# Sequential writes of the dilated heads' x, dilated masks spread on ScalarE, and a new table of due times

## The chip, the cores and the metric

The kernel runs on one core of a Trainium2 chip. The time is the device time of one execution in microseconds (us), lower is better; several executions are timed and their median is given. The engines are TensorE (PE; its weight loads are listed as PEld), VectorE (DVE), ScalarE (ACT), GpSimd (POOL) and SyncE (SP, which here issues the DMAs).

## The reference

Eight batches of 576 tokens, eight heads of 64. Heads 0 to 3 attend to a plain window of the last 32 tokens; heads 4 to 7 are dilated: they attend to every fourth token of the last 128. The concatenated heads go through a feed-forward block with a gate made by a three-tap convolution over tokens. All of it is float32.

```python
mask_plain = (rel >= 0) & (rel < 32)
mask_dil = (rel >= 0) & (rel < 128) & (rel % 4 == 0)
attn = softmax(where(mask, q @ k.T / 8, -1e9))
x = concat_heads(attn @ v)                 # (8, 576, 512)
h = relu(x @ w_in)                         # (8, 576, 1024)
gate = sigmoid(conv3(h, conv_w))           # taps at s-1, s, s+1
out = (h * gate) @ w_out                   # (8, 576, 512)
```

## The kernel before

**Attention.** A batch has four pairs of heads, p = 0 to 3; pairs 0 and 1 are plain (kind 0), pairs 2 and 3 dilated (kind 1). The host sorts the tokens of a dilated head by residue modulo 4, so that its window too becomes 32 neighbours. For a pair, `scores` (L255) issues 72 small matmuls into the PSUM buffer `att`, which is one buffer of four banks for the whole kernel; the add of the mask (L266) takes the scores out to SBUF, the softmax follows on VectorE and ScalarE (L268 to L289), a 32x32 transpose (L291) makes `pt`, and `values` (L307) issues 80 or 84 small matmuls into `att` again. `att` is free for the next pair when x has been taken out of it.

**Taking x out.** x is kept as two float32r tensors: x.t[0], names x0a to x6a in the trace, is the rounded value, and x.t[1], x0b to x6b, the rest. The cast at L330 (ACT) writes x.t[0] from PSUM. The rest is made in one of two ways. In batches 0 and 1 (`HELPED`), `less` (L334, PE) subtracts x.t[0] inside PSUM by matmuls with minus the identity, and a second ACT cast (L337) takes the difference out. In batches 2 to 7 one DVE subtraction (L342) reads PSUM and x.t[0] and writes x.t[1]. `made` gives the access patterns of all three. For a plain pair both sides are sequential. For a dilated pair PSUM holds the tokens by residue (four runs of 144) while x is in token order: the instruction walks PSUM in sequence and writes x in steps of four elements, 16 bytes.

**Feed-forward.** `expert` computes h by 192 matmuls of 288 columns per batch (L367), relu on ACT (L374), the convolution and the gate on ACT and DVE (L385, L379, L390, L392), splits the product in two (L394, L396), and multiplies by w_out with 512 columns (L412; 256 columns in batch 0); ACT copies the result (L422), SP stores it. Batches 0 and 1 take their exponentials slot by slot on ACT (L275, nine instructions a pair).

**Weights.** The weights arrive as 64-bit patterns in eight chunks (four of w_in, four of w_out) and `weights` converts each, with seven instructions on DVE and two on ACT (L476 to L491). PE can't begin a chunk of w_in before it is converted.

**Order.** `Planner` lays out all work before the kernel runs. Each step has an engine, a cost by the planner's own table and a due time from `DUE`. The planner repeatedly takes the engine that could start earliest and, of the steps that could start within 0.25 us of that, the one with the smallest due time. The order of instructions on each engine, SP's DMA queue included, is the sorted result. The planner's cost of a cast at L330 or L337 is 0.68 us and of the subtraction at L342 0.77 us, for plain and dilated pairs alike. `filled` puts matmuls of no use (L525) into PE's planned gaps between 5 and 31.5 us.

**Masks.** Before the planned work, small masks arrive by DMA (L497) and are spread over nine slots into `mask_sb` on DVE (L506 to L509), for both kinds.

Of the kernel before, what the change touches and what calls it, by code (L numbers as in the profile page):

```python
# [58 lines left out]
SCALE = 1.0 / D ** 0.5  # L59
SLOTS, HELPED = 0xff, 0xff  # L60
DUE = {
    "first": (157.10, 134.80, 52.00, 206.80, 505.80, -99.10, 677.00, 54.50),
    "gated": (199.50, 332.40, -57.10, -17.00, -100.80, -92.00, 541.40, -54.90),
    "second": (76.20, 952.70, 279.50, 455.50, 621.50, 924.90, 920.10, 207.80),
    "weights": (1282.30, 361.60, 883.70, 117.70, 161.40, 234.00, 242.00, 0.70),
    "fetch": (181.50, 89.90, 96.50, -94.10, 210.30, 760.90, 907.20, 915.10),
    "conv": 0.90,
    "scores": ((862.30, -93.20, -28.60, 858.10), (1.90, -187.00, -117.60, 119.50), (-13.20, 593.20, 765.10, 63.20), (141.00, -102.40, 265.70, -1.00), (184.00, 330.80, 18.90, 456.80), (229.10, 111.10, 305.10, 505.80), (620.00, 511.00, 783.60, 607.50), (932.70, -2.80, 494.20, 164.10)),
    "softmax": ((-34.40, -169.10, 49.00, 76.50), (-106.80, 15.70, 1.40, 96.40), (820.40, 925.10, 959.00, -67.90), (242.40, 566.70, -28.10, 230.90), (-66.40, 446.20, 40.30, 279.70), (632.70, 448.70, 871.10, -122.60), (592.80, -17.20, 875.60, -148.20), (-7.70, -174.00, 316.30, -52.10)),
    "values": ((120.70, -126.80, 16.90, -89.00), (-21.60, 21.90, -71.90, 35.70), (-22.30, -58.00, 92.90, -102.10), (140.70, -22.10, 73.40, 61.70), (468.60, 85.70, 99.50, 82.30), (184.50, -47.10, 183.70, 270.40), (284.30, 58.50, -77.80, 437.30), (-172.90, -95.90, 812.20, 434.80)),  # L70
    "queries": ((-134.90, -184.70, -104.20, -95.90), (-122.50, 4.80, 51.10, -59.30), (85.10, 70.50, -17.00, 144.40), (174.70, 186.60, 120.20, 157.10), (366.00, 234.00, 390.50, 255.70), (520.50, 532.70, 519.50, 248.70), (514.80, 543.20, 658.00, 446.80), (929.60, 882.70, 580.50, 835.90)),
    "runs": ((-56.90, -52.20, -66.80, -93.30), (68.20, -9.80, -23.30, -29.60), (80.40, 9.90, 147.40, 389.10), (498.10, 248.90, 25.00, 430.20), (635.00, 776.10, 449.50, 589.20), (922.60, 831.10, 869.40, 436.50), (1013.20, 1032.10, 1022.60, 620.40), (1268.60, 782.50, 987.10, 989.90)),
}


# [110 lines left out]
def attn_moe(ctx: ExitStack, tc: tile.TileContext, qk_p, qk_d, v_p, v_d, w_in, w_out, conv, mask, out):  # L186
    nc = tc.nc
# [49 lines left out]
    def attention(b, p):  # L237
        due, soft, val = SCORES[b][p], SOFTMAX[b][p], VALUES[b][p]
        kind = p // 2
        qk, v, s, m, z, pt, x = (Buffer(n) for n in ("qk", "v", "s", "m", "z", "pt", "x"))  # L240
# [3 lines left out]
            out=qk.t, in_=(qk_p, qk_d)[kind][b, p % 2]), uses=[qk])  # L244
        lv = plan.add("SP", 1.35, RUNS[b][p], lambda: nc.sync.dma_start(
            out=v.t, in_=(v_p, v_d)[kind][b, p % 2]), uses=[v])

        def scores():
# [18 lines left out]
            out=flat(), in0=scored(), in1=masked, op=ALU.add), [last], [sc, s])  # L267
        last = plan.add("DVE", 0.755, soft + 0.5, lambda: nc.vector.tensor_reduce(  # L268
            out=m.t, in_=flat(), axis=AX.X, op=ALU.max, negate=slotwise), [last], [s, m])
# [10 lines left out]
        else:  # L280
            last = plan.add("DVE", 0.755, soft + 1.0, lambda: nc.vector.tensor_tensor(
                out=flat(), in0=flat(), in1=wide(m.t), op=ALU.subtract), [last], [s, m])
            last = plan.add("ACT", 0.685, soft + 1.5, lambda: nc.scalar.activation(
                out=flat(), in_=flat(), func=AF.Exp, scale=SCALE), [last], [s], "exp")

            last = plan.add("DVE", 0.765, soft + 2.0, lambda: nc.vector.tensor_reduce(  # L286
                out=z.t, in_=s.t, axis=AX.X, op=ALU.add), [last], [s, z])
        last = plan.add("DVE", 0.215, soft + 2.2, lambda: nc.vector.reciprocal(out=z.t, in_=z.t), [last], [z])
        last = plan.add("DVE", 0.755, soft + 2.3, lambda: nc.vector.tensor_tensor(  # L289
            out=flat(), in0=flat(), in1=wide(z.t), op=ALU.mult), [last], [s, z])  # L290
        last = plan.add("DVE", 0.775, soft + 3.0, lambda: nc.vector.transpose(  # L291
            out=pt.t.rearrange("p (a k) -> p a k", k=W), in_=flat()), [last], [s, pt])
# [22 lines left out]
        def made(t):  # L315
            whole = tv.t.rearrange("p (c m) -> p c m", c=2)[:, :, TV0:TV0 + 2 * RUN]
            if kind == 0:
                return t.rearrange("p (c m) -> p c m", c=2), whole
            return t.rearrange("p (m c r) -> p c r m", c=2, r=2), whole.rearrange("p c (r m) -> p c r m", r=2)

        def spans():

            if kind == 0:
# [4 lines left out]
                    for c in range(2) for o, m, n in ((0, 0, RUN), (RUN, 0, 16), (RUN + 16, 16, RUN - 16))]  # L328

        last = plan.add("ACT", 0.68, val + 1.0, lambda: nc.scalar.copy(out=made(x.t[0])[0], in_=made(x.t[0])[1]), [last], [tv, x])  # L330
        if HELPED >> (b * NP + p) & 1:
            def less():
                for o, a in spans():
                    nc.tensor.matmul(tv.t[:, o:o + a.shape[1]], minus, a, start=False, stop=True, skip_group_check=True)  # L334

            last = plan.add("PE", 0.5, val + 1.2, less, [last], [tv, x], "E")
            return [plan.add("ACT", 0.68, val + 1.5, lambda: nc.scalar.copy(  # L337
                out=made(x.t[1])[0], in_=made(x.t[1])[1]), [last], [tv, x])]

        def low():  # L340
            out, whole = made(x.t[1])
            nc.vector.tensor_tensor(out=out, in0=whole, in1=made(x.t[0].bitcast(F32))[0], op=ALU.subtract)  # L342
# [153 lines left out]
    kinds_sb = cs[0][0].bitcast(BF16)[:, 0:5 * W].rearrange("p (a k) -> p a k", k=W)  # L496
# [5 lines left out]

    spread = lambda i, n: kinds_sb[:, i, :].unsqueeze(1).to_broadcast([128, n, W])
    slot_masks = [mask_sb[:, kind, :].rearrange("p (a k) -> p a k", k=W) for kind in range(2)]
    for t in slot_masks:
        nc.vector.tensor_copy(out=t, in_=spread(1, 9))  # L506
    nc.vector.tensor_copy(out=slot_masks[0][:, 0, :], in_=kinds_sb[:, 0, :])
    nc.vector.tensor_copy(out=slot_masks[1][:, 0, :], in_=kinds_sb[:, 2, :])
    nc.vector.tensor_copy(out=slot_masks[1][:, 4:6, :], in_=kinds_sb[:, 3:5, :])  # L509
    for t, in ss:  # L510
        nc.gpsimd.memset(t[:, :, W:W + 1], 1e-9)
    for h, in hs:
# [82 lines left out]
```

## Time and profile before

| | us |
|---|---|
| median of 3 runs (lowest to highest) | 525.82 (525.22 to 526.34) |
| the profiled execution, own time | 525.44 |
| its span, first to last instruction | 523.6 |
| busy PE / PEld / DVE / ACT in the span | 505.0 / 438.8 / 397.2 / 310.7 |

The span is taken from the profiled execution, whose own time is 1.84 us longer than its span and 0.38 us under the median. Busy times count an engine as busy while an instruction of it runs; matmuls are pipelined, so a busy PE isn't PE at its peak. The chain of waits is followed back from the last instruction to what released each step.

### The profile page before, as it was taken

The page shows a single profiled execution, that of the slowest core. Times are in us where ns is not written, and L with a number is a line of the kernel's source. Part 1 is how long each engine was busy: PE and PEld are TensorE (multiplying, and loading weights), DVE is VectorE, ACT ScalarE, POOL GpSimd, SP SyncE. Part 2 cuts the span into 40 slices and gives each one's busy share as a digit, 9 for nine tenths or more (in the row PEclk, how much of TensorE's full clock was granted, in tenths as well). Part 3 has the DMA queues.
Part 4 walks back from the last instruction along what each step waited for, and adds up shares of the span by engine and source line. Part 5 has one row for each costly group of instructions (what it writes and reads, how often), then busy time and mean ns, then how long its engine had stood idle before and what let it go on. Part 6 is the DMA issues. An engine that isn't in the chain of part 4 may idle for free.

```text
span 523.6 us, 16676 instructions
## 1 busy us (share of the span) xinstructions
PE 505.0 (96%) x7541; PEld 438.8 (84%) x7541; DVE 397.2 (76%) x555; ACT 310.7 (59%) x619; POOL 1.4 (0%) x27
## 2 busy tenths in 40 slices
PE   5989989999999999999999999999999999999996
PEld 3568889999777997799878998789977799789985
DVE  4998889998986899549992899957998469327900
ACT  4978989748423885268731787348733378338710
POOL 1000000000000000000000000000000000000000
PEclk9999989999999999999999999999999999999999
DMA  7766540211255004211333332230143200110011
GB/s 296 277 216 234 188 141 30 94 42 45 93 168 183 31 1 161 103 50 49 105 130 111 111 129 79 80 140 2 48 144 124 101 1 1 41 41 1 1 50 52
DMA packets 16551, 50.99 MB, mean 97 GB/s; under 512 B 2016, under 2 KB 3168, under 8 KB 15456
## 3 DMA queue, kind: packets, MB, share of 16 engines
q1 hardware_dynamic: 16336, 49.84, 28.0%
q8 instruction: 59, 0.97, 0.8%
q10 hardware_dynamic: 144, 0.08, 0.1%
q14 instruction: 12, 0.10, 0.1%
HBM read 40.48 MB, written 9.44 MB: 95 GB/s over the span
## 4 chain that ended last, share of the span: by engine, by line
PE 78%; DVE 12%; ACT 8%; DMA 1%; issue 1%; DVEq 0%; ACTq 0%
PE mm L367 35%; PE nn L412 32%; PE att L307 5%; PE att L255 4%; DVE s L289 2%; DVE pt L291 1%; DVE m L268 1%; DVE s L266 1%; PE nn L367 1%; DMA qk<-in_qk_p_dram 1%; DVE z L286 1%; ACT c L390 1%; PE att L334 1%; ACT h L374 1%; ACT L390 1%
## 5 line engine op out<-in xcount | busy, mean ns | idle before, releaser
L412 PE MATMUL nn<-wo,g 128*128 128x512 f32 (+1 forms) x960 | 211.9, 374 | 0.5 <-DVE g L396 0.3
L412 PEld LDWEIGHTS nn<-wo,g 128*128 128x128 f32 x960 | 163.7, 188 | 32.1 <-ACT g L394 0.7
L379 DVE SCALAR_TENSOR_TENSOR c<-h,conv_sb,c 128x576 f32<-128x576 f32 x128 | 102.9, 814 | 27.4 <-ACT c L385 25.9
L374 ACT ACTIVATE h<-mm 128x288 f32<-128x288 f32 x120 | 48.2, 407 | 34.4 <-PE mm L367 34.1
L422 ACT COPY out<-nn 128x512 f32<-128x512 f32 (+1 forms) x40 | 21.8, 544 | 65.6 <-PE nn L412 62.7
L367 PE MATMUL mm<-x0a,wi 128*128 128x288 f32 x208 | 59.1, 299 | 0.4 <-ACT h L374 0.4
L392 DVE TENSOR_TENSOR c<-c,h 128x576 f32<-128x576 f32 x64 | 47.9, 756 | 8.5 <-ACT c L390 8.0
L394 ACT CAST g<-c 128x576 fp32r<-128x576 f32 x64 | 42.8, 672 | 18.9 <-DVE c L392 18.8
L396 DVE TENSOR_TENSOR g<-c,g 128x576 fp32r<-128x576 f32 x64 | 47.6, 755 | 4.2 <-ACT g L394 2.8
L367 PE MATMUL mm<-x1a,wi 128*128 128x288 f32 x176 | 50.0, 300 | 0.2 <-ACT h L374 0.2
L385 ACT ACTIVATE c<-h,conv_sb 128x576 f32<-128x576 f32 x64 | 49.1, 777 | 1.5
L390 ACT ACTIVATE c<-c 128x576 f32<-128x576 f32 x64 | 43.2, 683 | 6.7 <-DVE c L379 5.7
L307 PEld LDWEIGHTS att<-pt,v 32*64 32x64 f32 x2624 | 31.5, 133 | 13.4 <-issue 4.4
L255 PEld LDWEIGHTS att<-qk 64*32 64x32 f32 x2304 | 26.5, 108 | 17.3 <-DMA qk<-in_qk_p_dram 5.3
L367 PEld LDWEIGHTS mm<-x0a,wi 128*128 128x128 f32 x208 | 39.0, 188 | 1.7 <-ACT h L374 1.3
L255 PE MATMUL att<-qk 64*32 64x64 f32 x2304 | 31.7, 230 | 7.5 <-DMA qk<-in_qk_p_dram 5.3
L307 PE MATMUL att<-pt,v 32*64 32x64 f32 (+1 forms) x2624 | 35.1, 233 | 2.7 <-DVE x5b L342 0.9
L266 DVE TENSOR_TENSOR s<-att,mask_sb 128x576 f32<-128x576 f32 x32 | 24.0, 751 | 17.9 <-PE att L255 17.8
L367 PE MATMUL mm<-x5a,wi 128*128 128x288 f32 x128 | 35.9, 295 | 0.0
L367 PE MATMUL mm<-x4a,wi 128*128 128x288 f32 x128 | 35.9, 295 | 0.0
L367 PEld LDWEIGHTS mm<-x1a,wi 128*128 128x128 f32 x176 | 33.0, 188 | 1.5 <-ACT h L374 0.9
L367 PE MATMUL mm<-x2a,wi 128*128 128x288 f32 x112 | 31.5, 297 | 0.0
(122 smaller groups left out, 813.2 us busy)
## 6 DMA issues: line engine op xcount, KB each, us to landing
qk<-in_qk_p_dram SPq DMA_DIRECT2D x16, 592.0 KB, 4.0
qk<-in_qk_d_dram SPq DMA_DIRECT2D x16, 592.0 KB, 4.1
out_dram<-out SPq DMA_DIRECT2D x28, 256.0 KB, 2.2
v<-in_v_d_dram SPq DMA_DIRECT2D x16, 384.0 KB, 3.7
v<-in_v_p_dram SPq DMA_DIRECT2D x16, 384.0 KB, 3.6
raw<-in_w_in_dram SPq DMA_DIRECT2D x4, 1024.0 KB, 6.4
raw<-in_w_out_dram SPq DMA_DIRECT2D x4, 1024.0 KB, 7.3
out_dram<-out SPq DMA_DIRECT2D x16, 128.0 KB, 2.4
```

The lines of the kernel that those rows point to most:

```text
L255: nc.tensor.matmul(sc.t[quad * 32:quad * 32 + 32, o:o + W], qk.t[hd * 64:hd * 64 + 64, q0:q0 + 32], qk.t[hd * 64:hd * 64 + 64, S + q0:S + ...
L266: last = plan.add("DVE", 0.75, soft + 0.0, lambda: nc.vector.tensor_tensor(out=flat(), in0=scored(), in1=masked, op=ALU.add), [last], [sc, s])
L307: nc.tensor.matmul(tv.t[hd * 64:hd * 64 + 64, o:o + hi - lo], v.t[quad * 32:quad * 32 + 32, i, hd * 64:hd * 64 + 64], pt.t[quad * 32:quad ...
L367: nc.tensor.matmul(ps.t[:, 0:HALF], wi[jw][fc // 2][:, fc % 2, k], x[k].t[jx][:, hf * HALF:hf * HALF + HALF], start=(k == 0 and i == 0), s ...
L374: relu.append(plan.add("ACT", 0.4, due + 1.6 * u + 1.6, lambda fc=fc, hf=hf, ps=ps: nc.scalar.activation(out=h[fc].t[:, 1 + hf * HALF:1 + ...
L379: nc.vector.scalar_tensor_tensor(out=c[fc].t, in0=h[fc].t[:, k:S + k], scalar=conv_sb[:, k, fc:fc + 1], in1=c[fc].t, op0=ALU.mult, op1=ALU ...
L385: t = plan.add("ACT", 0.777, d, lambda fc=fc: nc.scalar.activation(out=c[fc].t, in_=h[fc].t[:, 1:S + 1], func=AF.Copy, scale=conv_sb[:, 1, ...
L390: t = plan.add("ACT", 0.686, d + 1.0, lambda fc=fc: nc.scalar.activation(out=c[fc].t, in_=c[fc].t, func=AF.Sigmoid), [t], [c[fc]], "sigmoid")
L392: t = plan.add("DVE", 0.755, d + 1.5, lambda fc=fc: nc.vector.tensor_tensor(out=c[fc].t, in0=c[fc].t, in1=h[fc].t[:, 1:S + 1], op=ALU.mult ...
L394: hi = plan.add("ACT", 0.675, d + 2.0, lambda fc=fc: nc.scalar.copy(out=half(fc, 0), in_=c[fc].t), [t, *(done[fc] if odd else [])], [c[fc] ...
L396: lo = plan.add("DVE", 0.755, d + 2.5, lambda fc=fc: nc.vector.tensor_tensor(out=half(fc, 1), in0=c[fc].t, in1=half(fc, 0).bitcast(F32), o ...
L412: nc.tensor.matmul(ps.t[:, 0:n], g[k // 2].t[:, k % 2, jg, c0:c0 + 128], w.rearrange("p h c -> p (h c)") if hf is None else w[:, hf], star ...
```

## The change

Three edits. In `made` the dilated pattern turns its loops: x is walked in sequence (token group m, bank half c, residue r) and PSUM in steps: two elements 144 apart, then the same in the other bank half, then on to the next m. The three users of `made`, L330, L337 and L342, change with it; L334 doesn't. Second, the spreading of the masks is split: the plain masks stay on DVE (two instructions), the dilated ones (three instructions) go to ACT. Third, every value of `DUE` is new; no cost in the planner changes.

```diff
 DUE = {
-    "first": (157.10, 134.80, 52.00, 206.80, 505.80, -99.10, 677.00, 54.50),
+    "first": (74.70, 81.70, 357.10, 189.80, 929.80, 83.60, 71.70, 1180.10),
...
-    "weights": (1282.30, 361.60, 883.70, 117.70, 161.40, 234.00, 242.00, 0.70),
-    "fetch": (181.50, 89.90, 96.50, -94.10, 210.30, 760.90, 907.20, 915.10),
-    "conv": 0.90,
+    "weights": (82.70, 1550.20, 2380.40, 91.90, 97.30, -18.10, 171.90, 69.10),
+    "fetch": (69.90, 42.80, -64.40, -60.40, 72.60, 97.70, 1233.60, 1550.60),
+    "conv": 351.60,
...
             if kind == 0:
                 return t.rearrange("p (c m) -> p c m", c=2), whole
-            return t.rearrange("p (m c r) -> p c r m", c=2, r=2), whole.rearrange("p c (r m) -> p c r m", r=2)
+            return t.rearrange("p (m c r) -> p m c r", c=2, r=2), whole.rearrange("p c (r m) -> p m c r", r=2)
...
-    for t in slot_masks:
-        nc.vector.tensor_copy(out=t, in_=spread(1, 9))
-    nc.vector.tensor_copy(out=slot_masks[0][:, 0, :], in_=kinds_sb[:, 0, :])
-    nc.vector.tensor_copy(out=slot_masks[1][:, 0, :], in_=kinds_sb[:, 2, :])
-    nc.vector.tensor_copy(out=slot_masks[1][:, 4:6, :], in_=kinds_sb[:, 3:5, :])
+    for copy, t, changed in ((nc.vector.tensor_copy, slot_masks[0], ((0, 0, 1),)),
+                             (nc.scalar.copy, slot_masks[1], ((0, 2, 1), (4, 3, 2)))):
+        copy(out=t, in_=spread(1, 9))
+        for slot, i, n in changed:
+            copy(out=t[:, slot:slot + n, :], in_=kinds_sb[:, i:i + n, :])
```

## Rows read from the trace of the kernel before

**Rows 1.** The page, busy us of each engine over the span.
```profile
PE 505.0 (96%) x7541; PEld 438.8 (84%) x7541; DVE 397.2 (76%) x555; ACT 310.7 (59%) x619; POOL 1.4 (0%) x27
```

**Rows 2.** Windows: stretch, length, busy us (instructions) by engine, clock, DMA share, GB/s.
```profile
0.00:80.00 80.00, 69.39 (x1544) 54.11 (x1545) 66.55 (x99) 64.51 (x214) 1.41 (x27) 0.98 0.64 226
80.00:520.00 440.00, 435.64 (x5999) 384.72 (x5998) 330.69 (x457) 245.86 (x406) 0.00 (x0) 1.00 0.23 74
```

**Rows 3.** Chain of waits in the head: start us, length us, engine, tile, line.
```profile
35.31 1.21 ACT x2a L330
...
...
72.70 1.24 ACT x6b L337
```

**Rows 4.** Tiles: duration ns lowest/median/highest of the casts and subtractions.
```profile
L330 ACT CAST x0a<-att x7: 622/639/1198, 27.6 to 464.6; 128x576 fp32r<-128x576 f32 x7
...
L330 ACT CAST x3a<-att x4: 1167/1189/1232, 39.9 to 394.4; 128x576 fp32r<-128x576 f32 x4
...
L342 DVE TENSOR_TENSOR x0b<-att,x0a x5: 719/758/1172, 164.5 to 465.2; 128x576 fp32r<-128x576 f32 x5
...
L342 DVE TENSOR_TENSOR x3b<-att,x3a x3: 1133/1148/1154, 161.0 to 397.2; 128x576 fp32r<-128x576 f32 x3
...
L337 ACT CAST x2b<-att x1: 1240/1240/1240, 37.5 to 37.5; 128x576 fp32r<-128x576 f32 x1
```

**Rows 5.** PE's waits, 5 to 80 us: who waited for what: us, times, longest.
```profile
PE att L334 <- ACT x2a L330: 0.8, 1, 0.8
PE nn L367 <- ACT h L374: 0.8, 1, 0.8
...
PE att L334 <- ACT x4a L330: 0.3, 1, 0.3
```

**Rows 6.** PE's waits, 80 to 523.6 us, same columns.
```profile
PE att L307 <- DVE x5b L342: 0.9, 1, 0.9
...
PE att L307 <- DVE x3b L342: 0.2, 1, 0.2
```

**Rows 7.** PE in order of time around 74 us: start, length, instruction.
```profile
74.58 0.44 PE L367 MATMUL nn<-x0b,wi 128*128 128x288 f32 x1
74.82 0.44 PE L367 MATMUL nn<-x0a,wi 128*128 128x288 f32 x1
...
77.78 0.30 PE L367 MATMUL nn<-x2b,wi 128*128 128x288 f32 x1
77.92 0.29 PE L367 MATMUL nn<-x2a,wi 128*128 128x288 f32 x1
```

**Rows 8.** Granted clock, stretch of 5 us (columns as in Rows 2).
```profile
75.00:80.00 5.00, 4.45 (x102) 3.90 (x101) 2.90 (x5) 3.92 (x7) 0.00 (x0) 0.73 0.38 133
```

**Rows 9.** All engines in order of time at the start.
```profile
5.32 1.34 PE L255 MATMUL att<-qk 64*32 64x64 f32 x72 [5.32 <-DMA qk<-in_qk_p_dram]
5.47 0.81 DVE L506 COPY mask_sb<-c 128x576 bf16<-128x576 bf16 x2 [5.47 <-DMA c<-in_mask_dram]
...
6.69 0.76 DVE L266 TENSOR_TENSOR s<-att,mask_sb 128x576 f32<-128x576 f32 x1
...
8.27 0.21 ACT L271 ACTIVATE m<-m 128x9 f32<-128x9 f32 x1 [5.31 <-DVE m L268]
...
14.48 0.72 DVE L266 TENSOR_TENSOR s<-att,mask_sb 128x576 f32<-128x576 f32 x1
```

**Rows 10.** Groups by line and shape: busy us, mean ns, idle before.
```profile
L525 PE MATMUL nn<-eye 128*128 128x512 bf16 x77 | 18.6, 391 | 0.0
...
L482 DVE SCALAR_TENSOR_TENSOR t<-raw,t 128x1024 int32<-128x1024 int32 x8 | 9.8, 1224 | 0.2
...
L476 ACT ACTIVATE t<-raw 128x1024 f32<-128x1024 f32 x8 | 9.3, 1159 | 0.1
...
L477 DVE TENSOR_SCALAR t<-t 128x1024 f32<-128x1024 f32 x8 | 5.5, 688 | 0.5 <-ACT t L476 0.5
...
L484 ACT CAST wi<-t 128x1024 fp32r<-128x1024 f32 x4 | 4.3, 1065 | 0.8 <-DVE t L482 0.8
```

More of the change, by code (lines that the diff above doesn't have):

```diff
@@ L61 @@
 DUE = {
-    "first": (157.10, 134.80, 52.00, 206.80, 505.80, -99.10, 677.00, 54.50),
-    "gated": (199.50, 332.40, -57.10, -17.00, -100.80, -92.00, 541.40, -54.90),
-    "second": (76.20, 952.70, 279.50, 455.50, 621.50, 924.90, 920.10, 207.80),
-    "weights": (1282.30, 361.60, 883.70, 117.70, 161.40, 234.00, 242.00, 0.70),
-    "fetch": (181.50, 89.90, 96.50, -94.10, 210.30, 760.90, 907.20, 915.10),
-    "conv": 0.90,
-    "scores": ((862.30, -93.20, -28.60, 858.10), (1.90, -187.00, -117.60, 119.50), (-13.20, 593.20, 765.10, 63.20), (141.00, -102.40, 265.70, -1.00), (184.00, 330.80, 18.90, 456.80), (229.10, 111.10, 305.10, 505.80), (620.00, 511.00, 783.60, 607.50), (932.70, -2.80, 494.20, 164.10)),
@@ L69 @@
-    "softmax": ((-34.40, -169.10, 49.00, 76.50), (-106.80, 15.70, 1.40, 96.40), (820.40, 925.10, 959.00, -67.90), (242.40, 566.70, -28.10, 230.90), (-66.40, 446.20, 40.30, 279.70), (632.70, 448.70, 871.10, -122.60), (592.80, -17.20, 875.60, -148.20), (-7.70, -174.00, 316.30, -52.10)),
-    "values": ((120.70, -126.80, 16.90, -89.00), (-21.60, 21.90, -71.90, 35.70), (-22.30, -58.00, 92.90, -102.10), (140.70, -22.10, 73.40, 61.70), (468.60, 85.70, 99.50, 82.30), (184.50, -47.10, 183.70, 270.40), (284.30, 58.50, -77.80, 437.30), (-172.90, -95.90, 812.20, 434.80)),
@@ L71 @@
-    "queries": ((-134.90, -184.70, -104.20, -95.90), (-122.50, 4.80, 51.10, -59.30), (85.10, 70.50, -17.00, 144.40), (174.70, 186.60, 120.20, 157.10), (366.00, 234.00, 390.50, 255.70), (520.50, 532.70, 519.50, 248.70), (514.80, 543.20, 658.00, 446.80), (929.60, 882.70, 580.50, 835.90)),
-    "runs": ((-56.90, -52.20, -66.80, -93.30), (68.20, -9.80, -23.30, -29.60), (80.40, 9.90, 147.40, 389.10), (498.10, 248.90, 25.00, 430.20), (635.00, 776.10, 449.50, 589.20), (922.60, 831.10, 869.40, 436.50), (1013.20, 1032.10, 1022.60, 620.40), (1268.60, 782.50, 987.10, 989.90)),
+    "first": (74.70, 81.70, 357.10, 189.80, 929.80, 83.60, 71.70, 1180.10),
@@ new lines @@
+    "gated": (93.60, 342.20, 358.10, 9.30, 1117.90, -60.20, -25.30, 36.00),
+    "second": (24.50, 424.40, 452.80, 855.50, 1126.50, 1620.90, 1602.90, 1506.70),
+    "weights": (82.70, 1550.20, 2380.40, 91.90, 97.30, -18.10, 171.90, 69.10),
+    "fetch": (69.90, 42.80, -64.40, -60.40, 72.60, 97.70, 1233.60, 1550.60),
+    "conv": 351.60,
+    "scores": ((20.00, 1789.40, 129.10, 41.40), (1611.70, 17.90, -51.70, 73.80), (403.50, 353.80, 96.90, 65.70), (270.80, 69.10, 12.90, 80.10), (837.10, -73.40, 77.90, 140.80), (49.80, 977.60, -11.00, 940.00), (1183.10, 95.90, -34.70, 1535.50), (-103.80, 98.20, 411.50, 1557.60)),
@@ new lines @@
+    "softmax": ((6.00, -38.50, 7.80, 431.60), (-12.40, 25.50, 0.40, -12.70), (462.70, 1197.90, 365.00, 75.40), (1485.50, 93.40, -17.30, 1003.90), (41.70, 95.80, 1003.50, 910.00), (-44.30, 1543.80, 79.70, 1832.30), (155.80, 89.90, 461.20, 95.80), (94.80, 301.00, -37.60, 31.70)),
+    "values": ((842.50, -107.30, -8.70, 6.60), (-23.40, 4.00, 78.20, 43.70), (-4.50, -87.40, -34.50, 89.10), (3.90, 19.10, 32.20, 128.20), (29.70, 66.00, 347.10, -61.20), (-8.50, 1.60, 347.80, 17.20), (961.30, 71.70, 1044.10, 41.10), (22.90, 1623.60, 1475.90, 138.10)),
@@ new lines @@
+    "queries": ((-194.00, -340.50, -87.70, -64.20), (-95.90, 10.40, 59.30, -61.10), (22.90, 138.40, 114.70, 206.60), (959.30, 835.80, 807.00, 1024.00), (1038.20, 1322.20, 1022.30, 1286.00), (1424.90, 492.20, 1554.20, 1412.20), (1489.70, 1710.00, 973.30, 1772.10), (1810.40, 2547.40, 2385.70, 1573.80)),
+    "runs": ((-49.30, -20.50, -64.40, -5.70), (40.70, 36.00, 37.60, -38.70), (33.20, 97.00, 48.60, 47.50), (945.80, 351.90, 61.40, 98.30), (456.80, 1101.70, 167.50, 1221.90), (1380.70, 843.50, 1173.90, 1550.10), (1874.10, 1571.80, 1233.90, 1624.20), (1797.40, 2410.30, 1564.00, 1555.00)),
```

## The prediction

> **What bounds the kernel now.** The page comes first: PE is busy 96% of the span, its weight loads, which overlap, 84%, DVE 76%, ACT 59% [rows 1]. The windows split this [rows 2]: from 80 to 520 us PE is idle for 440 - 435.6 = 4.4 us only. In the first 80 us PE looks busy for 69.4, but 18.6 us of that are the matmuls of no use at L525 [rows 10], and DVE (66.6) and ACT (64.5) are nearly as full; this is the stretch where attention of the first batches and the conversion of weights keep PE short of work. So there are two places to gain: the head, where a late step on ACT or DVE delays everything behind it, and the rest, where only PE's idle 4.4 us are on offer.
>
> Then the chain of waits in the head: between 35 and 74 us it runs through eight casts of dilated pairs, four at L330 and four at L337, the first and last of which are shown [rows 3]. The tile view shows why they stand out [rows 4]. A plain pair's cast at L330 takes 0.64 us (x0a, whose one dilated case is the highest value), a dilated pair's 1.19 there (x3a, dilated all four times) and 1.24 at L337. The DVE subtraction takes 0.72 to 0.76 plain and 1.15 dilated. Shape, types and the sequential PSUM side are the same, so the excess (0.55, 0.60, 0.40) belongs to the 16-byte steps on x.
>
> **The sequential pattern: what an instruction costs after.** No row shows PSUM read in steps by ACT or DVE. Lower end: the plain pair's 0.64 and 0.72 [rows 4]. Upper end: the dilated 1.19 to 1.24 and 1.15, that is, the steps in PSUM cost what the steps in SBUF cost, or somewhat more, since every element now comes from another place. The nearest row for a stepped read is L476, which reads SBUF in steps of 8 bytes: 1.16 us for 1024 elements, where the cast of as many in sequence at L484 takes 1.07 [rows 10]; a stepped read cost 0.1 us there, not half a microsecond. I take 0.65 on ACT and 0.76 on DVE.
>
> [...]
>
> **The head.** 32 instructions of dilated pairs change: 4 + 4 casts in batches 0 and 1, 12 casts and 12 subtractions later. On the chain the eight head casts shrink by 4 x 0.55 + 4 x 0.60 = 4.6 us. PE can gain only where it stood idle for them. In the head's list of PE's waits seven are for these casts, from 0.8 us (x2a) to 0.3 (x4a), 3.5 us together, and an eighth of 0.8 is for a relu that stood behind the last of them on ACT [rows 5]. Taking for each the smaller of its idle time and its cast's saving gives 3.8 us. If DVE, busy for 66.6 of these 80 us, is the next to be late, half of it is lost: 1.9. I take 3.8.
>
> [...]
>
> **After 80 us.** Five of PE's waits lie behind a dilated subtraction: x5b 0.9, x0b 0.9, pt 0.6 (a transpose queued on DVE behind a dilated subtraction), x2b 0.3 and x3b 0.2, 2.9 us together; the first and the last are shown [rows 6]. A pair's cast and subtraction together shrink by 0.95, which covers each. The other dilated pairs end while PE has other matmuls, and what they win is worth nothing there. I take 2.8; with half-free instructions it would be 1.5.
>
> **Masks.** Taking three of five copies off DVE ends its part about 0.55 us earlier, at 6.05 instead of 6.6. But the first mask add starts at 6.69 because the first scores end at 5.32 + 1.34 = 6.66 [rows 9]: no gain. On ACT three copies wait for the mask's DMA at 5.47 and take at most some 1.5 us (576 elements like a plain cast, 0.64, and two small ones under 0.4). ACT's next instruction waits until 8.27 [rows 9], so they end in its idle time and delay no one; without that cover, an earlier step on ACT would slip by up to 1.5 us. The third mask add, the first that can be a dilated one, is at 14.5 [rows 9]. Cost: 0.
>
> **Due times.** The new table reorders every queue, SP's fetches included, so the waits above won't return in the same places. Bounds: downward, PE's remaining idle after 80 us is 4.4 - 2.9 = 1.5, and in the head DVE's idle 13.4 less the first 5.5 leaves about 8 that a better order could close [rows 2, 9]. Upward, a chunk of weights converted late costs DVE 3 x 1.22 + 4 x 0.69 = 6.4 us [rows 10]. One thing argues for a small gain: the planner charges 0.68 and 0.77 for all casts and subtractions, wrong by 0.5 for dilated pairs before and about right after, so a planned order will be kept better. I take 1.0 us of gain, a choice between wide ends.
>
> **Sum.** 3.8 + 0.8 + 2.8 + 0 + 1.0 = 8.4 us off the profiled execution's 525.44 gives 517.0. That execution lay 0.38 under the median, so 517.4 is forecast.
>
> **Rivals.**
> Steps in PSUM cost as much as steps in SBUF. Against it: the cheap stepped read at L476. For it: that row steps by 8 bytes in SBUF, here the steps are 576 bytes and a change of bank in PSUM. The three terms that rest on it (7.4) vanish and the order's 1.0 stays: 525.82 - 1.0 = 524.8, and some above the old time if the steps cost more. Chance 0.17 (about 0.05 faster, 0.07 same, 0.05 slower).
>
> The instructions shrink but the head doesn't: DVE, busy for 66.6 of 80 us [rows 2], paces it by conversions and softmax. Then 1.9 of 3.8, none of the clock, 1.5 of 2.8 and nothing from the order: 525.82 - 3.4 = 522.4. Chance 0.16.
>
> The new order starves PE in the head, which ends slower. Place: DVE's queue, where w_in's chunks 1 and 2 now have due times of 1550 and 2380, behind every softmax of the first batches, while chunks of w_out have 97 or less. PE has all of its useful work in the head from converted chunks of w_in. Price: 6.4 us of DVE for each conversion that something else gets ahead of. It decides when more than 8.4 us, 1.3 conversions, fall into PE's way; with two it is 525.8 - 7.4 + 12.8 = 531.2. Against it: in the table of before w_in's chunks 0, 2 and 1 also had late dues (1282, 884, 362), and a due time ranks only steps that could start within 0.25 us. Chance 0.12.
>
> The order wins much more, by DVE's 8 us of idle time in the head: 510 to 512. Chance 0.09.
>
> **How the numbers follow.** The forecast itself (513.5 to 520.5) has 0.46. The range 510 to 526 takes in all but the starved order and a little below, 0.84 together. With 0.2%, about 1 us, as what can be told from no change, faster is 0.46 + 0.16 + 0.09 + 0.05 = 0.76, same 0.08 (0.07 and a little of the neighbours), slower 0.16.
>
> **What would show it.** In the trace of after, dilated casts at L330 and L337 near 0.65 us and subtractions near 0.76; if they stand at 1.1 or more, the first rival holds. No chain pieces of 1.2 us on x tiles before 80 us, a granted clock of 1.00 between 70 and 80, and PE saturated some 5 us earlier. PE's waits for x tiles after 80 us under 1 us together. ACT's mask copies between 5.5 and 7 us with the first mask add still at 6.7. If the instructions shrink as said and the time doesn't fall, the place to look is when the last chunk of w_in is converted and how long PE waits for it.

## The result and the profile after

| | before | after |
|---|---|---|
| median, us | 526.08 | 520.61 |
| ratio (95% interval) | | 0.9883 (0.9854 to 0.9912) |
| profiled execution, own time / span, us | 525.44 / 523.6 | 520.62 / 518.8 |

The change takes 1.2% off, about 5.5 us, where 8.4 were forecast. A second set of runs of the changed kernel (e10) gave 0.9911 (0.9887 to 0.9935).

The dilated instructions have become as short as the plain ones. The tile views of after (durations lowest/median/highest), which answer to [rows 4]; x3a and x3b are now the tiles of both kinds of pairs, and the highest value tells:

```profile
L330 ACT CAST x3a<-att x5: 639/641/644, 39.6 to 390.9; 128x576 fp32r<-128x576 f32 x5
...
L342 DVE TENSOR_TENSOR x3b<-att,x3a x4: 756/758/758, 152.7 to 391.6; 128x576 fp32r<-128x576 f32 x4
...
L337 ACT CAST x2b<-att x1: 642/642/642, 37.8 to 37.8; 128x576 fp32r<-128x576 f32 x1
```

The window of after behind the head, to be read beside [rows 2]; PE's last matmul ends at 514.75, 519.70 before:

```profile
80.00:515.00 435.00, 430.58 (x5960) 380.66 (x5958) 319.67 (x453) 238.87 (x403) 0.00 (x0) 1.00 0.23 74
```

From 80 us to its last matmul PE is idle for 514.75 - 80 - 430.58 = 4.2 us; before it was 519.70 - 80 - 435.64 = 4.1. The waits of [rows 6] are gone and others stand in their place. PE's waits of after from 80 us on:

```profile
PE att L255 <- DVE pt L291: 1.6, 1, 1.6
PE att L255 <- issue: 1.3, 2, 1.0
...
```

In the head the granted clock stays at 1.00 between 70 and 80 us, where [rows 8] had 0.73.

A measure of where time is won: the start, in each profile, of the n-th of the 2496 large matmuls (L367 and L412), counted from 0 and read from the trace; "before" is the time, the other columns the difference from it. Kernels with the due times of before issue them in the same order, so their columns compare step by step; for the others only the last rows and the neighbourhood of 192 (the end of the head) are comparable. Each column is one execution; two executions of the changed kernel differ by 2.4 us at 192 (see e9 to e11).

| n | before, us | after | e1 pattern only | e5 head only | e6 rest only | e9 mixed dues |
|---|---|---|---|---|---|---|
| 192 | 78.84 | -4.45 | -2.02 | -3.29 | -0.92 | -3.13 |
| 672 | 157.77 | -3.35 | -1.90 | -3.16 | -0.79 | -1.02 |
| 768 | 176.28 | -0.28 | -2.90 | -3.15 | -1.58 | -1.37 |
| 1440 | 311.44 | -7.07 | -3.75 | -3.00 | -2.88 | -3.54 |
| 1536 | 332.23 | -5.78 | -4.64 | -3.00 | -3.76 | -4.42 |
| 1920 | 418.59 | -6.02 | -6.01 | -2.91 | -5.19 | -5.83 |
| 2495 | 519.27 | -4.95 | -5.95 | -3.05 | -5.12 | -5.48 |

### The profile page after: what moved, and what is told of

Same layout as the page of the kernel before. It is cut to its first block, busy times and chain, and to the rows that moved or that the text cites. A ratio compares the mean times of both kernels' runs of the same rounds, so it can differ in the third digit from the quotient of the medians.

```text
span 518.8 us, 16673 instructions
## 1 busy us (share of the span) xinstructions
PE 502.6 (97%) x7542; PEld 438.9 (85%) x7542; DVE 389.4 (75%) x552; ACT 303.9 (59%) x624; POOL 1.4 (0%) x27
## 4 chain that ended last, share of the span: by engine, by line
PE 86%; DVE 5%; ACT 4%; DMA 4%; issue 1%; ACTq 0%
PE nn L412 37%; PE mm L367 34%; PE att L307 6%; PE att L255 5%; DMA qk<-in_qk_d_dram 2%; PE nn L367 2%; PE nn L525 1%; ACT c L390 1%; ACT L390 1%; DMA c<-in_mask_dram 1%; DMA v<-in_v_p_dram 1%; DVE s L289 1%; DVE pt L291 1%; PE att L334 1%; ACT h L374 0%
## 5 line engine op out<-in xcount | busy, mean ns | idle before, releaser
L412 PE MATMUL nn<-wo,g 128*128 128x512 f32 (+1 forms) x960 | 210.8, 374 | 0.0
L412 PEld LDWEIGHTS nn<-wo,g 128*128 128x128 f32 x960 | 164.6, 188 | 32.0 <-ACT out L422 0.4
L367 PE MATMUL mm<-x6a,wi 128*128 128x288 f32 x192 | 54.5, 298 | 0.2 <-ACT h L374 0.2
L367 PE MATMUL mm<-x3a,wi 128*128 128x288 f32 x144 | 40.8, 299 | 0.2 <-ACT h L374 0.2
L367 PE MATMUL mm<-x2a,wi 128*128 128x288 f32 x144 | 40.8, 299 | 0.0
L367 PE MATMUL mm<-x1a,wi 128*128 128x288 f32 x144 | 40.3, 296 | 0.0
L367 PEld LDWEIGHTS mm<-x6a,wi 128*128 128x128 f32 x192 | 36.1, 188 | 1.0 <-ACT h L374 0.4
L367 PE MATMUL mm<-x5a,wi 128*128 128x288 f32 x128 | 36.4, 299 | 0.2 <-ACT h L374 0.2
L367 PE MATMUL mm<-x0a,wi 128*128 128x288 f32 x112 | 31.7, 300 | 0.0
L367 PE MATMUL mm<-x6b,wi 128*128 128x288 f32 x96 | 28.4, 296 | 0.0
```

The source lines that it names most:

```text
L367: nc.tensor.matmul(ps.t[:, 0:HALF], wi[jw][fc // 2][:, fc % 2, k], x[k].t[jx][:, hf * HALF:hf * HALF + HALF], start=(k == 0 and i == 0), s ...
L412: nc.tensor.matmul(ps.t[:, 0:n], g[k // 2].t[:, k % 2, jg, c0:c0 + 128], w.rearrange("p h c -> p (h c)") if hf is None else w[:, hf], star ...
```

## The experiments

**e1: the pattern alone.**

```diff
-            return t.rearrange("p (m c r) -> p c r m", c=2, r=2), whole.rearrange("p c (r m) -> p c r m", r=2)
+            return t.rearrange("p (m c r) -> p m c r", c=2, r=2), whole.rearrange("p c (r m) -> p m c r", r=2)
```

> The kernel before with the sequential pattern for dilated pairs alone; masks and due times as before. Theory (the shorter instructions carry the gain): the order of instructions is that of before, the eight head casts give 3.8 us, the clock dip 0.8, PE's waits after 80 us 2.8, so 526.1 - 7.4 = 518.7, ratio near 0.986. Rival (the new order carries the gain and the shorter instructions are hidden): within 2 us of 526.1.

Measured: 519.5 us, ratio 0.9873 (0.9856 to 0.989). The pattern carries the whole gain. No difference between it and the changed kernel's 0.9883 can be told from these runs. From 80 us to its last matmul PE is idle for 1.0 us, against 4.1 before and 4.2 after:

```profile
80.00:513.70 433.70, 432.71 (x5984) 382.98 (x5982) 323.75 (x455) 237.49 (x401) 0.00 (x0) 1.00 0.23 75
```

**e2: pattern and masks, due times of before.** The edit is the pattern and the split of the masks.

> The sequential pattern and the masks split, due times as before. If the masks on ScalarE cost nothing: the time of the kernel with the pattern alone. Rival, seen in the trace of after: on ACT the three mask copies run ahead of the two copies of the identity, the first matmuls of no use wait for the identity until 7.1 us, and the second pair's scores behind them start at 8.5 instead of 8.0; then 0.3 to 0.6 us slower than the pattern alone.

Measured: 519.08 us, ratio 0.9858 (0.9838 to 0.9879). No difference from e1 that can be told.

**e3: the new due times alone.** The kernel before with the new `DUE`.

> The kernel before with the new due times alone; dilated casts still write x in steps, masks on VectorE. Theory: without the shorter instructions the new order wins little, 523 to 527. Rival (the order carries the gain): about 520.6. Third: the new order relies on the short casts and is slower than before, 527 or more.

Measured: 526.21 us, ratio 1.0000 (0.9985 to 1.0015). With the old casts the new due times neither win nor lose.

**e4: the changed kernel with all masks on VectorE.**

> The changed kernel with all mask copies back on VectorE. If masks cost nothing either way: 520.6. If the delayed identity costs PE its start of the second scores: 0.3 to 0.6 us faster than the changed kernel, 520.0 to 520.3, with the second scores starting near 8.0 us.

Measured: 520.26 us, ratio 0.9893 (0.9865 to 0.9921): no difference from the changed kernel that can be told. But the delay that e2's expectation describes is there. In the changed kernel, in order of time at the start (start, length, instruction), ACT takes the masks first, the identity waits behind them, the matmuls of no use wait for the identity and the second scores for those:

```profile
5.54 0.67 ACT L507 COPY mask_sb<-c 128x576 bf16<-128x576 bf16 x1 [3.08 <-DMA c<-in_mask_dram]
...
6.80 0.28 ACT L500 CAST eye<-pt 128x128 bf16<-128x128 f32 x1
...
7.14 1.46 PE L525 MATMUL nn<-eye 128*128 128x512 bf16 x3 [0.41 <-ACT eye L500]
...
8.53 1.22 PE L255 MATMUL att<-qk 64*32 64x64 f32 x72
```

In e4 the same two steps on PE:

```profile
6.62 1.46 PE L525 MATMUL nn<-eye 128*128 128x512 bf16 x3
8.02 1.33 PE L255 MATMUL att<-qk 64*32 64x64 f32 x72
```

In the kernel before, the cast that makes the identity (L500) runs at 2.68 us. In e4 the second scores start 0.5 us earlier than in the changed kernel; the time as a whole doesn't show it.

**e5 and e6: the pattern in the head alone, and in the rest alone.**

```diff
+            if b < 2:        # e5; b > 1 in e6
+                return t.rearrange("p (m c r) -> p m c r", c=2, r=2), whole.rearrange("p c (r m) -> p m c r", r=2)
             return t.rearrange("p (m c r) -> p c r m", c=2, r=2), whole.rearrange("p c (r m) -> p c r m", r=2)
```

> The kernel before with the sequential pattern for the dilated pairs of batches 0 and 1 alone (eight casts). Theory as predicted: 3.8 + 0.8 = 4.6 us off, ratio 0.991. Rival, after the first runs: the head carries nearly the whole 1.3% of the pattern, ratio 0.988 or less. Third: in the head DVE and PE's own instruction supply give it back, ratio above 0.994.

> The kernel before with the sequential pattern for the dilated pairs of batches 2 to 7 alone (12 casts, 12 subtractions). Theory as predicted: 2.8 us off, ratio 0.995. Rival: PE's waits there are taken over by the next step, ratio within 0.002 of 1.

Measured: e5 523.79 us, ratio 0.9960 (0.9940 to 0.9980); e6 521.42 us, 0.9914 (0.9897 to 0.9932). In us of 526 the head gives 2.1 (1.1 to 3.2) and the rest 4.5 (3.6 to 5.4); together 6.6, and e1 with both gave 6.7. The two terms of the forecast were the other way round.

**e7: what ate the head's gain.** In e1 PE stops for two microseconds in the middle of the sixth scores. The view of waits calls this "issue": PE waited for nothing that the view can name. PE in order of time in e1, with the wait in brackets:

```profile
41.30 0.64 PE L255 MATMUL att<-qk 64*32 64x64 f32 x38
...
43.97 0.76 PE L255 MATMUL att<-qk 64*32 64x64 f32 x34 [2.04 <-issue]
```

SP had issued the fourth chunk of w_in just before, and the windows of e1 (last three numbers: clock, DMA share, GB/s) show the DMA engines busy for 0.96 of the last two microseconds before the gap, and the clock at 0.52 behind it:

```profile
37.02 0.33 SPq L470 DMA_DIRECT2D raw<-in_w_in_dram  x1
```

```profile
40.00:42.00 2.00, 1.94 (x49) 1.61 (x48) 1.93 (x3) 1.41 (x2) 0.00 (x0) 1.00 0.96 381
42.00:44.00 2.00, 0.03 (x4) 0.03 (x4) 1.20 (x1) 1.47 (x2) 0.00 (x0) 1.00 0.11 37
44.00:46.00 2.00, 2.00 (x39) 1.83 (x40) 0.73 (x1) 0.21 (x1) 0.00 (x0) 0.52 0.19 39
```

In the kernel before, the same scores ran without a gap at 43.4, after that load. e7 is e1 with that one DMA moved two places down in SP's queue:

```diff
...
+        load, raw = loads[0]
+        at = todo.index(load)
+        todo.remove(load)
+        dmas = [i for i, t in enumerate(todo) if i >= at and t.engine == "SP"]
...
+        todo.insert(dmas[1] + 1, load)
...
```

> The kernel with the pattern alone stood idle on PE for 2.0 us in the middle of the sixth scores (after 38 of 72 matmuls, at 42 us) for nothing that the trace names, while the DMA engines carried the fourth chunk of w_in, issued at 37.0. Here that load alone is moved in SP's queue behind the fetch that waits for these scores. If PE's instructions arrive late because that load fills the DMA engines: the gap falls below 0.3 us and these scores end 1.5 to 2 us earlier; the fourth conversion starts about 5 us later, so the time as a whole may go either way, 518 to 523. If the gap has another cause: it stays near 2 us.

Measured: the gap is gone, all 72 matmuls of these scores run from 41.21 on in one piece. But ACT's first step of this chunk's conversion now waits 8.8 us for the load, until 51.04 (42.30 in e1), and relus stand behind it in ACT's queue. PE waits 8.6 us for one of them, and the time is 526.59 us, ratio 1.0013 (0.9998 to 1.0028). PE of e7, and its longest wait:

```profile
41.21 0.97 PE L255 MATMUL att<-qk 64*32 64x64 f32 x72
```

```profile
PE mm L368 <- ACT h L375: 8.6, 1, 8.6
```

So the gap depends on that load. The trace also has transfers whose times fit it. Among the DMA packets are packets of instructions; those on queue 8, 59 of 16 KB each in the kernel before, keep step with PE: the packet after the one that matters here starts at the 894th to 897th matmul (all of PE's counted, from 0) in e1, e2, e5, e6, e7, e11 and the kernel before, and the next in e7 only at 58.72 us, after PE's long wait. The DMA view of e1 from 41 to 43 us:

```profile
q8 instruction: 1, 0.02, 3.0%
```

The times of that packet, read from the trace, beside PE's (us); the gap lies before the 859th matmul in all profiles that have one:

| | PE reaches matmul 806 | packet starts | ends | matmul 859 starts | gap before it |
|---|---|---|---|---|---|
| before | 40.31 | 40.96 | 41.91 | 43.83 | none |
| e6 | 40.21 | 41.04 | 41.97 | 43.71 | none |
| e7 | 39.24 | 39.22 | 40.14 | 41.61 | none |
| e1 | 39.31 | 41.71 | 42.66 | 43.97 | 2.04 |
| e5 | 39.10 | 41.43 | 42.37 | 43.82 | 2.10 |
| e11 | 39.11 | 41.06 | 41.99 | 43.37 | 1.64 |
| after | 39.87 | 41.13 | 42.10 | 43.33 | 0.72 |

Wherever there is a gap, PE goes on 1.2 to 1.5 us after the packet has ended; the same holds in e2, e4, e8, e9 and e10. Without the load in the way (e7) the packet starts when PE reaches its 806th matmul; with it, 0.7 to 2.4 us later. No view names what PE waited for; the reading that fits is that PE ran out of instructions, because their packet came late beside the load. Why the delay differs from profile to profile no run shows. The changed kernel has the gap too, only shorter.

**e8: x written two elements at a time.**

```diff
-            return t.rearrange("p (m c r) -> p c r m", c=2, r=2), whole.rearrange("p c (r m) -> p c r m", r=2)
+            return t.rearrange("p (m c r) -> p c m r", c=2, r=2), whole.rearrange("p c (r m) -> p c m r", r=2)
```

> The pattern alone, but with the PSUM bank half as the outer loop: x is written two elements at a time (8 of every 16 bytes), PSUM read in pairs 144 apart within one bank half. If it is the stepping over 16 bytes for every single element that costs: casts near 0.65 us and the time of the pattern alone, ratio 0.987. If anything but a sequential write pays: casts at 0.8 to 1.2 us and a ratio above 0.99.

Measured: 518.92 us, ratio 0.9869 (0.9849 to 0.9889), like e1. Its casts (tile view, as above), x3a dilated each time:

```profile
L330 ACT CAST x3a<-att x4: 647/671/704, 39.0 to 389.9; 128x576 fp32r<-128x576 f32 x4
L342 DVE TENSOR_TENSOR x3b<-att,x3a x3: 720/721/723, 159.3 to 392.6; 128x576 fp32r<-128x576 f32 x3
```

For 576 elements, two in every 16 bytes cost ACT 0.03 us over the sequential write (0.67 against 0.64) and DVE nothing (0.72 against the plain 0.72 to 0.76); one in every 16 bytes cost 0.55 and 0.40.

**e9 to e11: is the new order good for anything?** e9 has the pattern, the new due times for batches 0 and 1, weights, fetches and the weights of the convolution, and the due times of before plus 200 for the rest. e10 and e11 repeat the changed kernel and the pattern alone beside it.

> The pattern alone with a mixed table: the new due times for batches 0 and 1, weights and fetches, the due times of before, each raised by 200, for batches 2 to 7. In the profiles the changed kernel is 2.5 us ahead of the pattern alone by the 192nd of the big matmuls and 1 us behind it at the end. If the new order wins in the head and loses later: about 2 us faster than the pattern alone, near 517. If the two halves can't be joined without new waits at the seam: 518 to 521.

> The changed kernel beside the pattern alone on one chip. If the new order and the masks together are worth nothing: both ratios within 0.002 of each other, near 0.988.

> The pattern alone, beside the changed kernel. If the new order and the masks together are worth nothing: within 0.002 of its ratio. If the old order is the better one with short casts: 0.001 to 0.003 below it, as the first runs had it (0.9873 against 0.9883).

Measured on one chip: e11, the pattern alone, 518.59 us, 0.9850 (0.9825 to 0.9874); e9 520.27 us, 0.9882 (0.9857 to 0.9907); e10, the changed kernel, 522.21 us, 0.9911 (0.9887 to 0.9935). With e1 and the first runs of the changed kernel, the old order is ahead twice, once clear of the noise (e11 against e10). These pairs differ in the masks as well, but the masks alone changed nothing that can be told (e2 against e1, e4 against the changed kernel), so the difference is put down to the order. The mixture doesn't join the good halves: at the 192nd large matmul it is 1.1 us ahead of e1, at the last 0.5 behind.

The head's part in this varies between executions. In the first profile of the changed kernel the 192nd large matmul starts 4.45 us earlier than before, in e10's, the same kernel, only 2.01; the pattern alone has 2.02 (e1) and 2.62 (e11). From 80 us to PE's last matmul the two orders differ in the same way both times: PE is idle for 4.2 and 3.3 us with the new one, for 1.0 and 1.0 with the old. The window of e10:

```profile
80.00:516.50 436.50, 433.16 (x5978) 383.32 (x5976) 322.06 (x456) 241.02 (x406) 0.00 (x0) 1.00 0.23 76
```

No version is faster than the smallest edit, the pattern alone (e1, e11): it beats the kernel before both times and the changed kernel in the comparison that is clear of the noise; e2 and e8 can't be told from it.

## Why the prediction came out as it did

**Instruction lengths: right.** Steps of 576 bytes and changes of bank in PSUM cost nothing that shows here: 0.64 on ACT, 0.72 to 0.76 on DVE, at or near the lower ends of the bounds. The first rival falls for reads by ACT and DVE. That the excess belonged to the 16-byte steps on x is borne out by e8 (0.67 us on ACT with two elements in every 16 bytes, 1.19 before with one).

**The head: mechanism right, sized too large.** 3.8 + 0.8 were forecast, e5 gave 2.1. Of PE's 3.5 us of idle time behind the casts 0.5 is left in e5; what failed is the step "PE can gain only where it stood idle for them", which asked what PE waited for and not what it would run into by coming 2 us earlier. By the times of e7's table PE came to instructions whose packet had not landed (in e5 PE stops at 41.72 us, the packet ends at 42.37), late beside a load of weights; in the kernel before, PE got there 1.9 us after the packet's end. That is the gap of 2.0 us (2.1 in e5), which e7 takes away by moving one load. The rival that had the head paced by DVE got the amount (1.9 of 3.8) but not the reason.

**The clock: a term that comes and goes.** No run shows the 0.8 of the sum; it was the author's estimate for the dip of the granted clock in the kernel before, 0.58 from 74 to 76 us and 0.57 from 76 to 78 [rows 7, 8]. What the runs show in its place: the dip is gone in the profiles of after, e1 and e5 (1.00 from 70 to 80 us), as forecast. But it is gone in e6's too (1.00 from 70 to 80 us), whose casts in the head are those of before, so the shorter casts need not be the reason:

```profile
75.00:80.00 5.00, 4.44 (x110) 4.03 (x109) 3.81 (x6) 4.99 (x9) 0.00 (x0) 1.00 0.41 134
```

The profiled execution of before, with its dip, has a mean granted clock of 0.997, and of the 22 executions of the kernel before that were timed beside e5, 12 have 0.999 or more: by that mean they had no such dip to lose. In e1 the clock falls to 0.52 behind the new gap, and all five executions have a mean of 0.997 or 0.998. In e5 seven executions of eleven have 0.996 or 0.997 and take 523.35 to 525.61 us; four have 1.000 and take 522.26 to 523.36. The profile of e5 is one of the four, with the gap and without a dip, so the 3.05 in the table's last row is its better case; the median gives 2.1. The 0.8 was not a gain that could be counted on.

**After 80 us: mechanism right, sized too small.** 2.8 forecast, 4.5 (3.6 to 5.4) measured in e6, 4.2 in its profile behind the 192nd matmul. The forecast counted only the waits that name a dilated tile or a queue seen to stand behind one. The table shows one that was missed: between the 1440th and the 1536th matmul e6 wins 0.9 us. There, in the kernel before, a dilated subtraction stood on DVE in front of a step of the gate for which PE then waited (DVE in order of time, kernel before):

```profile
324.80 1.20 DVE L342 TENSOR_TENSOR x6b<-att,x6a 128x576 fp32r<-128x576 f32 x1 [0.54 <-ACT x6a L330]
...
327.40 0.76 DVE L396 TENSOR_TENSOR g<-c,g 128x576 fp32r<-128x576 f32 x1
```

The matmuls of L412 waited 0.5 us there for steps of the gate (0.3 and 0.2), the weight loads 1.3. PE's idle time from 80 us to its last matmul fell by 3.3 us in e6, to 0.7, which is 0.5 more than the forecast's 2.8:

```profile
80.00:514.55 434.55, 433.83 (x5993) 384.13 (x5991) 324.81 (x457) 238.45 (x403) 0.00 (x0) 1.00 0.23 75
```

The last 0.9 of the 4.2 is no idle time of matmuls; no run shows what it is. The 4.5 may also hold some of the head's clock: the profile of e6 is 0.9 us ahead at the 192nd large matmul, though no changed instruction runs before it.

**Masks: the sum right, the reasoning short.** Nothing measurable, as forecast. But "they end in its idle time and delay no one" looked only at ACT's next planned step. The identity, made at 2.68 us before, got behind the copies, which wait for the masks' DMA, and PE's second scores start 0.5 us later.

**Due times: a gain that didn't come, and probably the wrong sign.** 1.0 us of gain was taken on the argument that the planner's costs become right and a planned order is kept better. With the old casts the new table is worth nothing (e3); with the new ones the changed kernel is behind the pattern alone by 0.001 in one comparison, which is noise, and by 0.006 in the other. Most of what it lacks is lost behind the head, where PE's idle time is 3.3 to 4.2 us instead of 1.0. That the right costs helped the old order as well, and so left nothing to the new one, is a reading that no run tests. The rival in which the new order starves PE in the head didn't occur: at the 192nd large matmul both profiles of the changed kernel are ahead of before. Nor does e7 price it, though its 7 us against e1 are close to the rival's 6.4 for a chunk. There it was ACT, not DVE's queue, that held PE up, and the granted clock from 44 to 54 us was 0.65.

**The sum.** 8.4 forecast, 5.5 measured. The pattern's three terms were forecast at 7.4 together and measured at 6.7 (e1), by two errors that nearly cancel: 2.5 too much in the head, 1.7 too little behind it. That they nearly cancel is luck. The rest of the difference is the order: 1.0 forecast, a loss of 0.5 (not told from nothing) to 3 measured, masks included.

## What to carry to other kernels

Where a permutation can sit on either side of a PSUM evacuation, try the steps on the PSUM read and write SBUF in sequence: here the instruction went from 1.19 to 0.64 us on ACT and from 1.15 to 0.76 on DVE, the length of a plain one. A new table of due times that comes with such an edit should be measured apart from it; here the old order with the new instructions was at least as fast, and in one comparison clearly faster. When a step in the start of a kernel gets shorter, look at which transfers the earlier work will now run beside, not only at the waits it removes; in e1 a packet of instructions came late beside such a transfer, and PE stood still for 2.0 us.

## What was not expected of the hardware

ACT and DVE read PSUM element by element, 576 bytes apart and across banks, in the time of a sequential read (0.64 and 0.72 to 0.76 us for 576 elements, in the profile of after as in plain pairs before). A write of 576 elements, two in every 16 bytes of SBUF, takes 0.67 us on ACT (e8), one in every 16 bytes 1.19 (before). Packets of instructions that keep step with PE, 16 KB each, are among the DMA packets (59 on queue 8 in the kernel before). Beside a 1 MB load one such packet started 2.0 to 2.4 us after PE reached the point where it started without that load (e1, e5, e11 against e7), and PE stood still for 1.6 to 2.1 us, until 1.3 to 1.5 us after the packet's end.
